# A fused attention and mixture-of-experts kernel: gathers of the second expert block behind two scatters, and a new engine order of the last six pairs and the first expert block

## The chip, the cores and the metric

The kernel runs on one core of a Trainium2 chip. The metric is the device time of one launch in microseconds (us), given as the median of several runs. One further execution was recorded by the hardware profiler; its rows are what the prediction argues from. Five engines work side by side, each with its own list of instructions: PE multiplies matrices, ACT (Activation) and DVE (Vector) work on elements, POOL (GpSimd) does the same and issues the gathers and scatters, and SP issues the plain transfers. In the profile, PEld is PE's loading of weights.

## The reference

The reference first computes attention and then sends every token of its output through one of eight small networks ("experts"):

```python
# attention: 8 batches, 8 heads, 576 positions, 64 values per head
q_rot, k_rot = rotate(q), rotate(k)
scores = scale * q_rot @ k_rot^T
scores = scores - max(scores)
attn = exp(scores); attn = attn / (sum(attn) + 1e-9)
x = (attn @ v), reshaped to 4608 tokens of 512 values
# experts: 8 of them, 512 -> 1024 -> 512
logits = x @ w_gate + modality_bias[modality_id]
e_idx = argmax(logits, axis=1)
gate_w = softmax(logits)[e_idx]
for e in range(8):
    h = relu(x[e_idx == e] @ w1[e])
    out[e_idx == e] = gate_w * (h @ w2[e])
```

## The kernel before

**Attention.** The 64 heads are done as 32 pairs, numbered 0 to 31, four pairs to a batch. For each pair there are nine blocks of scores (jobs S0 to S8, matmuls at L472), each followed by a row minimum on DVE that also copies the scores out of PSUM (MN, L481) and an exponential on ACT (EX, L490). The exponentials are then transposed on PE (the "fills" F0 to F3, FA and FB, L495) into PSUM, and brought out of PSUM half by ACT and half by DVE (A_ and B_ jobs, L432 and L528). Then come the products with V (AVA and AVB, L553), a copy of their result on ACT (OTA, OTB), the output matmuls (OUT, L590) and their evacuation on DVE (EVA, EVB, L603 to L607). A pair's jobs reach over some three periods, so that PE works on two or three pairs at once.

**PSUM.** There are four slots of two banks, ps0 to ps3. A job takes the slot that a table names for it, or the one that came free longest ago, and so a job in written order can only start when the slot's last reader has read it.

**Routing.** After the last pair of a batch the routing steps RK0 to RK14 find each token's expert (on PE one short group of matmuls, RK8 at L675 and L677, and small steps on ACT, DVE and POOL), and five scatters SC0 to SC4 on POOL write the tokens' numbers into a table in device memory (TAB<-VAL, L708).

**Experts.** Tokens are handled in blocks of 256. Eight blocks of the first plan hold tokens of batches 0 to 4 only, so that they can begin before the last batches are routed; ten more and a half block follow. For each block SP reads the block's list of tokens (ix and xi), POOL gathers the rows (8 gathers per block, XG0 or XG1 by turns, L970, in the job rows), DVE and ACT transpose and split them (tr, te, L1015), ACT and DVE split the weights (hi, lo, hi2, lo2), and PE does the two layers (l1 at L1034, l2 at L1053).

**What sets the order.** All of it is a list of small jobs. Each job has a key, and the list is sorted by key plus 14.438 times the pair's number. The table KEYS holds the keys that are the same for all pairs, EDGE replaces them pair by pair, and MOE holds the keys of the first expert blocks, relative to pair 31. PE, ACT, DVE and POOL execute their instructions in exactly the order that the sorted list gives, and so does SP until the list ends; nothing is put in another order later. After the list the rest of the expert blocks follow in an order that the code writes out (chain). A second small table, AFTER, ties five gathers of the first block to matmuls of pair 30: two to the first half of its product with V, two to the second half and one to its output matmuls. So these gathers are issued as PE gets on.

In the new kernel the lines of the code stand 18 lines further down: L472 is L490 there, L495 is L513, L553 is L571, L590 is L608, L675 is L693, L708 is L726, L970 is L988, and L1034 is L1052.

Of the kernel before, what the change touches and what calls it, by code (L numbers as in the profile page):

```python
# [84 lines left out]
        -104.800, "OTA": -100.434, "A_F3": -91.502, "B_F3": -82.128, "AVB": -67.882, "RI": -64.058, "OTB": -58.510, "OUT": -54.919,  # L85
        "EVA": -46.469, "EVB": -43.282,
    },
# [9 lines left out]
        "BIAS": -0.898, "EVA": 4.373, "EVB": 9.686, "RK0": 17.329,  # L97
    },
# [9 lines left out]
    },  # L108
# [5 lines left out]
    },  # L114
    6: {
        "LD1": -117.371, "T1": -115.739, "LD": -91.534, "T2": -87.025, "R": -60.217, "HI": -56.245, "LO": -39.229, "SWH": -29.499,
        "SWL": -25.629,
    },
    7: {
        "LD": -77.705, "LD1": -51.155, "T1": -45.849, "T2": -29.455,  # L120
    },
    8: {
        "LD1": -42.214,
    },
    19: {
        "SC3": 113.825, "SC2": 128.215, "SC4": 152.075,
    },
    23: {
        "RK6": 45.016, "RK7": 49.391, "RK8": 52.824, "RK9": 58.160, "RK10": 79.988, "RK11": 109.721, "RK12": 128.347, "RK13": 128.956,
        "RK14": 129.684, "SC3": 130.859, "SC4": 132.359, "SC2": 132.942, "SC1": 136.961, "SC0": 137.506,  # L130
    },
    25: {
        "RE": 11.575, "F2": 13.246, "A_F2": 14.351, "B_F2": 14.486, "RI": 16.427, "AVB": 18.725, "OTB": 20.519, "OUT": 26.426, "EVB":
        26.591, "EVA": 30.118,
    },
# [57 lines left out]
    },  # L193
}
MOE = dict(
    setdma=(-353.070, -199.654, -64.082, -129.156),
    consts=(28.166, 28.282),
    plan=(-34.727, 11.672, -5.857, -25.884),
    ix=(-13.525, 11.677, 11.679, 11.775),
    w1=(-33.501, -27.735, 15.231, -22.655),  # L200
    w2=(-4.011, 1.762, 12.647, -8.483),
    hi=(-22.046, 1.027, 19.870, 16.903),
    lo=(17.011, 6.975, 21.263, 19.523),
# [1224 lines left out]
```

## Time and profile before

| what | us |
|---|---|
| median of the three runs | 916.37 |
| lowest and highest of the three | 913.91 and 916.81 |
| time of the profiled execution | 911.67 |
| its span from the first to the last instruction | 909.9 |
| PE busy in that span | 863.7 (95%) |
| DVE busy | 685.8 (75%) |
| ACT busy | 632.3 (69%) |
| POOL busy | 641.1 (70%) |

The mean clock that PE was granted in the span is 0.985 of full speed. The profiled execution's own time is 1.8 us above its span. A row of the timeline gives the start, the duration, the engine, the line of the code, the operation, the result and its sources, and the number of instructions that were put together; in brackets stands the time that the engine was idle before it and what ended that time. "issue" there means that the engine waited for nothing that the profile shows. A row of the windows gives the busy time of PE, PEld, DVE, ACT and POOL in one stretch (with the number of instructions), PE's granted clock, the share of the DMA engines' time and the rate in GB/s.

### The profile page before, as it was taken

How to read it: one execution, taken by the hardware profiler on the slowest of the kernel's cores; microseconds unless marked ns; L12 is line 12 of the kernel's file. 1: busy time of each engine (PE TensorE's matmuls, PEld its weight loads, DVE VectorE, ACT ScalarE, POOL GpSimd, SP SyncE). 2: the span in 40 equal slices, each digit the busy share in tenths (PEclk: the TensorE clock that was granted, in tenths of full speed). 3: DMA queues.
4: the chain of work that ended last, by engine and by line, in shares of the span. 5: the costliest groups of instructions: out<-in, count | busy, mean ns of one | idle time of the engine just before them, and what ended most of it. 6: DMA issues, size and time to landing. Idle time of an engine off the chain costs nothing. (4 is left out here: it accounts for less than half of the span.)

```text
span 909.9 us, 25743 instructions
## 1 busy us (share of the span) xinstructions
PE 863.7 (95%) x9696; PEld 715.4 (79%) x9696; DVE 685.8 (75%) x1515; ACT 632.3 (69%) x1291; POOL 641.1 (70%) x494
## 2 busy tenths in 40 slices
PE   2899999999999999999869989999999999999996
PEld 2677777777777777777648978889999999999995
DVE  7788889888888889888739767857676666666672
ACT  2888988888988988989734545556556555555563
POOL 3999988998889999995551776765666666666401
PEclk9999999999999999999969999999999999999999
DMA  8675778788797787867601611116717112511250
GB/s 263 200 225 156 247 180 219 182 207 204 151 246 181 190 207 182 230 166 215 171 21 67 222 49 46 54 59 228 237 55 229 47 47 88 192 46 38 81 171 20
DMA packets 82465, 136.90 MB, mean 150 GB/s; under 512 B 28795, under 2 KB 53517, under 8 KB 81308
## 3 DMA queue, kind: packets, MB, share of 16 engines
q1 hardware_dynamic: 71740, 114.08, 46.5%
q0 software_dynamic: 9248, 19.46, 6.6%
q8 instruction: 78, 1.28, 0.6%
q10 hardware_dynamic: 1344, 1.62, 0.6%
q14 instruction: 55, 0.45, 0.2%
HBM read 138.16 MB, written 19.51 MB: 173 GB/s over the span
## 5 line engine op out<-in xcount | busy, mean ns | idle before, releaser
L481 DVE CUSTOM_DVE_ANT_1 sc<-ps,ZERO 128x576 f32<-128x576 f32 x288 | 206.8, 749 | 23.3 <-PE ps L472 13.0
L490 ACT ACTIVATE P<-sc,mn 128x576 f32<-128x576 f32 x288 | 219.7, 767 | 5.8 <-DVE mn L481 5.2
L970 POOL DMA_INDIRECT XG<-X,iy x148 | 174.6, 1180 | 48.5 <-issue 37.6
L1034 PE MATMUL psH<-HL,W1H 128*128 128x256 f32 x1088 | 194.6, 281 | 3.2 <-issue 2.9
L472 PE MATMUL ps<-SW 64*128 64x288 f32 x960 | 170.3, 312 | 15.8 <-DMA SW<-HL 14.9
L472 PE MATMUL ps<-HL 64*128 64x288 f32 x960 | 170.6, 311 | 3.2 <-DVE ri L573 1.1
L1034 PEld LDWEIGHTS psH<-HL,W1H 128*128 128x128 f32 x1088 | 168.1, 189 | 4.0 <-issue 1.9
L1034 PE MATMUL psH<-HL,W1L 128*128 128x256 f32 x544 | 152.8, 281 | 0.9 <-issue 0.9
L472 PEld LDWEIGHTS ps<-SW 64*128 64x128 f32 x960 | 136.2, 190 | 20.6 <-DMA SW<-HL 15.9
L429 DVE TENSOR_TENSOR W1L<-ST,W1H 128x1024 fp32r<-128x1024 f32 x76 | 90.3, 1222 | 76.3 <-ACT W1H L432 65.5
L472 PEld LDWEIGHTS ps<-HL 64*128 64x128 f32 x960 | 136.2, 190 | 8.6 <-issue 5.5
L553 PE MATMUL ps<-PH,V 128*64 128x320 f32 (+1 forms) x1024 | 140.9, 416 | 2.2 <-issue 1.2
L1057 POOL DMA_INDIRECT out_dram<-sc,ix x36 | 47.0, 1305 | 115.3 <-ACT sc L1056 94.0
L495 PEld LDWEIGHTS ps<-idf,P 64*128 64x128 f32 x2624 | 96.8, 139 | 32.7 <-ACT P L490 12.1
L432 ACT ACTIVATE PH<-ps 128x512 f32<-128x512 f32 (+1 forms) x160 | 85.3, 551 | 48.5 <-PE ps L495 25.0
L528 DVE COPY PH<-ps 128x512 f32<-128x512 f32 (+1 forms) x160 | 98.4, 630 | 26.6 <-remote 12.8
L495 PE MATMUL ps<-idf,P 64*128 64x64 f32 x2624 | 109.1, 226 | 6.9 <-issue 3.5
L1053 PE MATMUL psY<-W2L,SW 128*128 128x512 f32 x288 | 113.7, 395 | 0.0
L1053 PE MATMUL psY<-W2H,SW 128*128 128x512 f32 x288 | 112.3, 390 | 0.0
L553 PEld LDWEIGHTS ps<-PH,V 128*64 128x64 f32 x1024 | 69.7, 137 | 51.3 <-issue 6.0
L449 POOL TENSOR_TENSOR HL<-ST,HL 128x1152 fp32r<-128x1152 f32 x31 | 82.4, 2657 | 36.6 <-ACT HL L432 36.5
L1034 PEld LDWEIGHTS psH<-HL,W1L 128*128 128x128 f32 x544 | 102.9, 189 | 3.8 <-issue 3.7
(216 smaller groups left out, 1596.7 us busy)
## 6 DMA issues: line engine op xcount, KB each, us to landing
ST<-in_moe_w_dram SPq DMA_DIRECT2D x152, 512.0 KB
ST<-in_qk_dram SPq DMA_DIRECT2D x62, 576.0 KB
SW<-HL SPq DMA_DIRECT2D x124, 216.0 KB
V<-in_v_dram SPq DMA_DIRECT2D x32, 256.0 KB
X<-X SPq DMA_DIRECT2D x8, 1024.0 KB
XG<-X,iy POOLq DMA_INDIRECT x148
V<-in_v_dram SPq DMA_DIRECT2D x64, 16.0 KB
X<-XT SPq DMA_DIRECT2D x16, 64.0 KB
```

What stands on the lines that cost most here:

```text
L429: nc.vector.tensor_tensor(o, a, b, op=ALU.subtract)
L432: return nc.scalar.activation(o, i, AF.Copy, scale=scale)
L449: e.tensor_tensor(d["HL"][:, 1, o], a, d["HL"][:, 0, o].bitcast(F32), op=ALU.subtract)
L472: nc.tensor.matmul(ps[:, g, 0:288], t[:, wq, q0:q0 + P], t[:, wk, k0:k0 + 288], start=(m == 0), stop=(m == len(L) - 1))
L481: nc.vector.tensor_tensor_reduce(sc, d.pop(("S", u))[:, :, 0:288], ZERO.unsqueeze(2).to_broadcast([P, 2, 288]), 1.0, FMAX, ALU.add, ALU.mi ...
L490: nc.scalar.activation(p, sc.rearrange("p a b -> p (a b)"), AF.Exp, bias=mn, scale=-1.0, accum_out=d["sum"][:, u:u + 1])
L495: nc.tensor.transpose(ps[:, g, c:c + 64], src[r, k0:k0 + P], idf[r, r])
L528: alone(d["at", f], g, (nc.vector.tensor_copy if g else acopy)(o, i).ins)
L553: i = nc.tensor.matmul(pa[hh * 64:hh * 64 + 64, 0:c1 - c0], d["V"][:, hh, kt, :], r, start=(kt == 0), stop=(kt == 4))
L970: inst = nc.gpsimd.indirect_dma_start(out=XG[s % 2][:, t, g, :], out_offset=None, in_=X.rearrange("n (i f) -> (n i) f", f=P)[0:rows], in_o ...
L1034: l1_[s] = nc.tensor.matmul(ps[:, i, :], w[:, c, f0:f0 + P], x[:, c, :], start=(m == 0), stop=(m == 11)).ins
L1053: nc.tensor.matmul(ps, hx[:, c, t * P:(t + 1) * P], x[:, c, :], start=(m == 0), stop=(m == 23))
```

## The change

The change is one of tables, with one small change of code.

- In EDGE the numbers of pairs 0 to 22 are printed with more digits and are the same. Those of pair 23 (its routing steps), 24 (two), 25 and all of 26 to 31 are new, and so PE, ACT, DVE and POOL run these pairs' jobs in another order. The first job that differs is near the start of pair 26's scores, which PE works on at about 364 us of the profiled span.
- In MOE the eight gathers of the second expert block (rows 8 to 15) go from keys 11.78 to 14.07 to keys 17.36 to 17.43, which is behind two scatters of batch 5 (SC3 and SC4 of pair 23). What they read, the block's list of tokens (plan 1, ix 1), goes from 11.67 to 16.18 and 17.30. The steps of the first block (hi, lo, tr, te, hi2, lo2, l1, l1e) have new keys too.
- `alone` declares that two users of one slot that work in different banks of it need not wait for each other. It now gets the half of the pair that each of them belongs to, and leaves the dependence in place where the half is the same.

On SP the order of the transfers is kept, but for the second block's plan and list, which now stand behind two weight loads, and the stores of the last batch, which stand behind two more. POOL issues the same gathers and scatters. Nothing is added and nothing removed: each engine has the same instructions.

The core of the diff (of the tables two or three lines each):

```diff
     31: {
-        "LD": -37.174, "T2": -35.339, "LD1": -34.769, "T1": -28.480, "R": -24.189, "HI": -20.952, "LO": -14.069, "SWL": -13.658, "SWH":
...
+        "LD": -37.17400, "LD1": -34.76900, "T2": -34.16480, "T1": -26.03419, "R": -22.15154, "HI": -21.41976, "LO": -19.21119, "SWL":
...
 MOE = dict(
-    plan=(-34.727, 11.672, -5.857, -25.884),
-    ix=(-13.525, 11.677, 11.679, 11.775),
+    plan=(-34.72700, 16.18300, -5.85700, -25.88400),
+    ix=(-13.52500, 17.30000, 11.67900, 11.77500),
...
-    rows=(5.189, -7.595, 2.778, 1.170, -0.984, 8.071, 5.429, 11.766, 11.780, 11.790, 14.020, 14.030, 14.040, 14.050, 14.060, 14.070,
+    rows=(5.18900, -7.59500, 2.77800, 1.17000, -0.98400, 8.07100, 5.42900, 11.76600, 17.36000, 17.37000, 17.38000, 17.39000, 17.40000,
...
-    def alone(own, b, inst):
+    def alone(own, b, inst, part=None):
 
-        for x, i in use[own]:
-            if x != b and i.engine != inst.engine:
+        for x, p, i in use[own]:
+            if x != b and i.engine != inst.engine and (p is None or p != part):
                 tc.declare_no_dep(inst, i, reason="two banks")
-        use[own].append((b, inst))
+        use[own].append((b, part, inst))
...
-            alone(d["at", f], g, (nc.vector.tensor_copy if g else acopy)(o, i).ins)
+            alone(d["at", f], g, (nc.vector.tensor_copy if g else acopy)(o, i).ins, int(f[1] in "23B"))
...
-                alone(own, half, i.ins)
+                alone(own, half, i.ins, half)
```

How the instructions stand at the two places that the prediction rests on is shown here. A row has the line, the operation, the result and its sources with their numbers, the size, and how often the instruction follows itself.

On PE, the end of pair 31's scores, before. P0 and P1 hold pair 31's exponentials, of which the rows at L495 are fills F1 and F0; oT is pair 30's product with V, and the rows at L675 are the first ones of RK8 of batch 6:

```order
L472 MATMUL ps3_130<-SW1_85 128x288
L495 MATMUL ps1_128<-idf_65,P1_119 128x64 x16
L590 MATMUL ps0_127<-RW_112,oT0_113 64x72 x18
L495 MATMUL ps3_130<-idf_65,P0_118 128x64 x16
L675 LDWEIGHTS UT_146
L675 MATMUL ps1_128<-OH_148,UT_146 128x48
```

and the same place on PE in the new kernel:

```order
L490 MATMUL ps0_127<-SW1_85 128x288
L513 MATMUL ps3_130<-idf_65,P0_118 128x64 x16
L608 MATMUL ps1_128<-RW_112,oT0_113 64x72 x18
L693 LDWEIGHTS UT_146
L693 MATMUL ps2_129<-OH_148,UT_146 128x48
```

Before, RK8 follows fills F1, OUT of pair 30 and fill F0, in slot ps1, which held F1; now it follows F0 and OUT of pair 30, in slot ps2, and F1 comes after it.

On POOL, the gathers of the first and second expert block (XG0 and XG1) and the scatters into the table, before:

```order
L970 DMA XG0_75<-X_63,iy_8540 128x128 x4
L962 TENSOR_SCALAR iy_8994<-xi_8981,CF_70 128x8
L970 DMA XG1_76<-X_63,iy_8994 128x128 x2
L689 TENSOR_TENSOR rk_8906<-rk_8906,OH_148 128x40
L970 DMA XG1_76<-X_63,iy_8994 128x128 x6
L697 CAST oi_9063<-of_9041 128x5
L708 DMA TAB_64<-VAL_71,oi_9063 41472x2 x5
```

and in the new kernel:

```order
L988 DMA XG0_75<-X_63,iy_8581 128x128 x7
L715 CAST oi_8986<-of_8709 128x5
L726 DMA TAB_64<-VAL_71,oi_8986 41472x2 x2
L980 TENSOR_SCALAR iy_9110<-xi_9108,CF_70 128x8
L988 DMA XG1_76<-X_63,iy_9110 128x128 x8
L726 DMA TAB_64<-VAL_71,oi_8986 41472x2
L638 COPY G_149<-BI_144 128x5x8
L726 DMA TAB_64<-VAL_71,oi_8986 41472x2 x2
L707 TENSOR_TENSOR rk_8882<-rk_8882,OH_148 128x40
```

Before, eight gathers of XG1 go ahead of all five scatters, and before them stand four gathers of XG0 in a row, the other four being issued further up, between small routing steps; now seven gathers of XG0 stand in a row, two scatters follow, then the eight gathers of XG1, and then the other three scatters.

More of the change, by code (lines that the diff above doesn't have):

```diff
@@ L115 @@
-    6: {
-        "LD1": -117.371, "T1": -115.739, "LD": -91.534, "T2": -87.025, "R": -60.217, "HI": -56.245, "LO": -39.229, "SWH": -29.499,
-        "SWL": -25.629,
[6 rows of a table added]
+        -378.64700, "LV": -364.17600, "FB": -346.46500, "A_FB": -336.88000, "B_FB": -329.74400, "AVA": -327.20100, "OTA": -302.11700,
+        "F3": -299.87500, "A_F3": -295.07300, "B_F3": -294.95300, "AVB": -234.67400, "OTB": -230.71800, "RI": -224.64500, "OUT":
+        -153.22800, "EVA": -132.78200, "EVB": -119.48400,
+    },
[9 rows of a table added]
+        -196.83900, "AVA": -190.98200, "OTA": -176.51300, "RE": -145.24400, "AVB": -140.63700, "RI": -126.46800, "OTB": -111.27300,
+        "OUT": -65.54500, "EVA": -42.99700, "EVB": -41.82000,
+    },
[8 rows of a table added]
+        "B_F2": -118.63100, "RE": -114.64700, "B_FB": -114.13100, "A_FB": -113.59600, "AVA": -109.96600, "F3": -104.80000, "OTA":
+        -100.43400, "A_F3": -91.50200, "B_F3": -82.12800, "AVB": -67.88200, "RI": -64.05800, "OTB": -58.51000, "OUT": -54.91900, "EVA":
+        -46.46900, "EVB": -43.28200,
+    },
[8 rows of a table added]
+        "FB": -51.27500, "A_FB": -49.23100, "AVA": -45.36800, "B_F2": -42.94200, "B_FB": -42.19100, "F3": -41.92200, "OTA": -41.65200,
+        "A_F2": -39.41600, "A_F3": -38.58300, "B_F3": -34.37400, "RE": -34.12100, "RI": -14.32900, "AVB": -13.48900, "OTB": -8.26400,
+        "OUT": -1.34400, "BIAS": -0.89800, "EVA": 4.37300, "EVB": 9.68600, "RK0": 17.32900,
+    },
[9 rows of a table added]
+        "AVB": 14.42600,
+    },
[6 rows of a table added]
+    },
@@ L118 @@
+    6: {
+        "LD1": -117.37100, "T1": -115.73900, "LD": -91.53400, "T2": -87.02500, "R": -60.21700, "HI": -56.24500, "LO": -39.22900, "SWH":
+        -29.49900, "SWL": -25.62900,
     },
     7: {
-        "LD": -77.705, "LD1": -51.155, "T1": -45.849, "T2": -29.455,
+        "LD": -77.70500, "LD1": -51.15500, "T1": -45.84900, "T2": -29.45500,
     },
     8: {
-        "LD1": -42.214,
+        "LD1": -42.21400,
     },
     19: {
-        "SC3": 113.825, "SC2": 128.215, "SC4": 152.075,
+        "SC3": 113.82500, "SC2": 128.21500, "SC4": 152.07500,
@@ L127 @@
     },
     23: {
-        "RK6": 45.016, "RK7": 49.391, "RK8": 52.824, "RK9": 58.160, "RK10": 79.988, "RK11": 109.721, "RK12": 128.347, "RK13": 128.956,
-        "RK14": 129.684, "SC3": 130.859, "SC4": 132.359, "SC2": 132.942, "SC1": 136.961, "SC0": 137.506,
+        "RK5": 40.90127, "RK6": 46.67389, "RK7": 57.40156, "RK8": 64.29648, "RK9": 67.61357, "RK10": 82.92576, "RK11": 85.53740, "RK12":
+        96.07624, "RK13": 114.20615, "RK14": 128.57076, "SC3": 130.85900, "SC4": 132.35900, "SC2": 132.94200, "SC1": 136.96100, "SC0":
@@ L131 @@
+        137.50600,
+    },
+    24: {
+        "EVB": 25.99150, "EVA": 26.06138,
     },
     25: {
-        "RE": 11.575, "F2": 13.246, "A_F2": 14.351, "B_F2": 14.486, "RI": 16.427, "AVB": 18.725, "OTB": 20.519, "OUT": 26.426, "EVB":
-        26.591, "EVA": 30.118,
+        "AVA": 10.88958, "FB": 12.15678, "B_FB": 13.12055, "OTA": 13.19636, "F2": 13.31092, "B_F2": 13.52622, "A_FB": 14.37274, "RE":
+        14.41030, "A_F2": 14.56559, "F3": 14.92462, "A_F3": 15.78341, "B_F3": 16.11466, "AVB": 16.75621, "RI": 18.17626, "OTB":
+        20.01352, "OUT": 27.50939, "EVB": 29.53316, "EVA": 29.76110,
@@ L135 @@
     },
     26: {
[5 rows of a table removed]
-        "OTB": 24.647, "RI": 27.870, "OUT": 31.453, "EVA": 32.577, "EVB": 35.739,
[6 rows of a table added]
+        "AVA": 13.37242, "B_F2": 14.18103, "OTA": 15.10887, "AVB": 20.37058, "OTB": 22.17156, "RI": 30.50016, "OUT": 33.13718, "EVA":
+        33.71284, "EVB": 36.68954,
     },
     27: {
[5 rows of a table removed]
-        "A_FB": 13.315, "B_FB": 14.059, "AVA": 14.280, "RE": 14.638, "A_F3": 14.844, "B_F3": 15.844, "OTA": 16.826, "AVB": 19.635,
[3 rows of a table removed]
[6 rows of a table added]
+        15.84080, "FB": 15.97787, "AVA": 16.14316, "A_FB": 16.77823, "OTA": 16.82819, "B_FB": 17.62644, "AVB": 20.22011, "OTB":
@@ L154 @@
+        21.83520, "OUT": 25.12055, "EVB": 25.68147, "EVA": 25.70549, "BIAS": 26.59725, "RK0": 27.27627, "RK1": 30.31245, "XO": 36.25000,
+        "RK2": 40.37238, "RK3": 43.17076, "RK4": 44.57894, "RK5": 48.83850, "RK6": 56.47619, "RK7": 56.55748, "RK8": 66.74962, "RK9":
+        67.91421, "RK10": 75.41390, "RK11": 81.11650, "RK12": 81.45284, "RK13": 82.49673, "RK14": 82.51116, "SC0": 83.05200,
     },
     28: {
[6 rows of a table removed]
-        "OTA": 17.939, "RE": 19.181, "AVB": 20.414, "OTB": 23.398, "RI": 25.977, "OUT": 38.336, "EVA": 39.257, "EVB": 40.186,
[7 rows of a table added]
@@ L163 @@
+        16.05280, "B_F3": 16.56402, "AVB": 19.82456, "OTB": 24.47882, "RI": 28.16419, "OUT": 37.99977, "EVA": 38.80736, "EVB": 40.35017,
     },
     29: {
[6 rows of a table removed]
-        "B_FB": 12.181, "OTA": 12.576, "RE": 12.876, "B_F3": 13.074, "RI": 13.187, "A_F3": 13.894, "AVB": 15.303, "OTB": 20.667, "OUT":
-        40.409, "EVA": 46.235, "EVB": 48.346,
[8 rows of a table added]
+        "EVB": 53.24566, "EVA": 53.43772,
     },
     30: {
[7 rows of a table removed]
-        21.050, "OUT": 21.663, "EVA": 37.670, "EVB": 37.831,
[7 rows of a table added]
+        12.05367, "A_F3": 12.41287, "B_F2": 12.87059, "A_FB": 13.34276, "B_FB": 14.29187, "AVB": 18.71721, "RE": 18.88984, "OTB":
@@ L183 @@
+        19.15819, "RI": 19.30164, "OUT": 22.05238, "EVB": 26.15506, "EVA": 32.21461,
     },
     31: {
[6 rows of a table removed]
-        12.309, "F2": 12.476, "B_FB": 12.480, "A_F2": 12.738, "AVA": 13.069, "B_F2": 13.586, "AVB": 16.396, "OTB": 23.586, "OTA":
-        23.807, "OUT": 24.531, "RI": 24.900, "EVA": 24.910, "EVB": 24.920,
[7 rows of a table added]
+        13.65186, "A_F3": 14.42523, "AVA": 15.43182, "AVB": 15.76070, "RE": 17.38437, "OTB": 18.55238, "OTA": 19.95731, "BIAS":
+        20.75437, "OUT": 24.42589, "RI": 24.90000, "EVA": 24.91000, "EVB": 24.92000,
@@ L195 @@
 MOE = dict(
-    setdma=(-353.070, -199.654, -64.082, -129.156),
-    consts=(28.166, 28.282),
-    plan=(-34.727, 11.672, -5.857, -25.884),
-    ix=(-13.525, 11.677, 11.679, 11.775),
[L200 to L203, printed above, removed]
-    tr=(13.315, 14.512),
-    te=(14.739, 14.961),
-    hi2=(19.097, 17.808, 17.228, 16.018),
-    lo2=(24.633, 22.805, 24.459, 19.614),
-    l1=(17.301, 17.002, 22.720, 21.734),
-    l1e=(22.809, 22.869, 24.662, 24.647),
-    w1n=(20.502, 24.643, 23.254, 22.825),
-    place=(10.490, 11.490),
-    rows=(5.189, -7.595, 2.778, 1.170, -0.984, 8.071, 5.429, 11.766, 11.780, 11.790, 14.020, 14.030, 14.040, 14.050, 14.060, 14.070,
-        25.150, 25.160, 25.170, 25.180, 25.190, 25.200, 25.210, 25.220),
-    pl=(-114.356, -102.856, -99.906, -88.406, -85.506, -73.956, -51.417, -48.907, -45.303),
+    setdma=(-353.07000, -199.65400, -64.08200, -129.15600),
+    consts=(28.16600, 28.28200),
+    plan=(-34.72700, 16.18300, -5.85700, -25.88400),
+    ix=(-13.52500, 17.30000, 11.67900, 11.77500),
+    w1=(-33.50100, -27.73500, 15.23100, -22.65500),
+    w2=(-4.01100, 1.76200, 12.64700, -8.48300),
+    hi=(-19.90978, 15.80757, 21.38490, 15.44691),
+    lo=(6.12812, 16.23179, 22.24599, 20.18067),
+    tr=(11.97182, 13.67190),
+    te=(14.33785, 14.80071),
+    hi2=(20.51992, 16.30432, 17.29412, 16.03064),
+    lo2=(23.20071, 17.00040, 22.32476, 20.98521),
+    l1=(15.78498, 17.03336, 23.35045, 22.37281),
+    l1e=(21.32014, 23.18167, 23.40073, 22.43414),
+    w1n=(20.50200, 24.64300, 23.25400, 22.82500),
+    place=(10.49000, 11.49000),
+    rows=(5.18900, -7.59500, 2.77800, 1.17000, -0.98400, 8.07100, 5.42900, 11.76600, 17.36000, 17.37000, 17.38000, 17.39000, 17.40000,
+        17.41000, 17.42000, 17.43000, 25.15000, 25.16000, 25.17000, 25.18000, 25.19000, 25.20000, 25.21000, 25.22000),
+    pl=(-114.35600, -102.85600, -99.90600, -88.40600, -85.50600, -73.95600, -51.41700, -48.90700, -45.30300),
     end=25.0,
```

7 lines of the change are left out of this document (removed), and 158 rows, old and new, of the table EDGE.

## The prediction

> **What bounds the kernel now.** The busy times of the page come first, then the chain of waits, to see from where on the end is fixed.
>
> ```profile
> PE 863.7 (95%) x9696; PEld 715.4 (79%) x9696; DVE 685.8 (75%) x1515; ACT 632.3 (69%) x1291; POOL 641.1 (70%) x494
> 575.75 11.36 PE psH L1034 x95
> 587.11 11.10 PE psY L1053 x48
> ...
> 877.28 11.10 PE psY L1053 x48
> ```
>
> PE is busy for 863.7 of 909.9 us, and from 575.75 us the chain is PE alone, one expert block after the other in 11.2 + 11.1 us. Nothing that the change moves stands there, so the end comes earlier only by as much as PE reaches 575.75 earlier. I therefore looked for PE's losses in the windows of the part that the change reorders, from about 364 us on.
>
> ```profile
> 364.00:420.00 56.00, 55.59 (x908) 42.77 (x910) 47.97 (x145) 49.67 (x131) 52.45 (x42) 1.00 0.74 196
> 420.00:440.00 20.00, 19.46 (x298) 14.41 (x296) 16.53 (x46) 18.52 (x48) 5.18 (x8) 1.00 0.74 199
> 440.00:445.00 5.00, 3.94 (x54) 2.88 (x51) 3.39 (x12) 2.66 (x8) 3.93 (x7) 1.00 0.79 209
> 445.00:450.00 5.00, 5.00 (x54) 3.27 (x56) 4.36 (x12) 4.36 (x11) 3.29 (x4) 1.00 0.51 117
> 450.00:455.00 5.00, 3.15 (x102) 2.74 (x100) 2.83 (x8) 3.45 (x11) 3.20 (x4) 1.00 0.75 241
> 455.00:460.00 5.00, 3.08 (x45) 2.04 (x39) 2.13 (x6) 1.25 (x4) 3.91 (x6) 0.60 0.19 47
> 460.00:465.00 5.00, 1.90 (x12) 1.25 (x11) 0.27 (x2) 0.00 (x0) 3.81 (x6) 0.50 0.18 48
> 465.00:470.00 5.00, 2.51 (x14) 1.30 (x14) 0.00 (x0) 0.00 (x0) 3.79 (x4) 0.50 0.02 1
> 470.00:475.00 5.00, 4.69 (x27) 3.50 (x29) 2.87 (x4) 3.42 (x5) 0.00 (x0) 0.70 0.01 0
> 475.00:480.00 5.00, 5.00 (x42) 4.41 (x39) 4.97 (x10) 5.00 (x6) 0.00 (x0) 1.00 0.00 0
> ```
>
> Up to 440 us PE is full (55.59 of 56.00, 19.46 of 20.00). After it there are short losses and then, from 455 to 475 us, a large one: PE is busy for 12.18 of 20 us, at a granted clock of 0.60, 0.50, 0.50 and 0.70. Busy time multiplied by clock is 1.85 + 0.95 + 1.26 + 3.28 = 7.3 us of full work, so some 12.7 us are lost. The waits, of the window from 440 to 476.5 us (engine, line, what it waited for, us in total, times, longest) and, in the last row, of PE from 364 to 440, say to what the losses are put down:
>
> ```profile
> PE ps L495 <- issue: 3.5, 6, 1.0
> PE ps L590 <- issue: 3.0, 6, 1.1
> PE ps L675 <- ACT PH L432: 1.8, 1, 1.8
> PE ps L553 <- issue: 1.2, 2, 0.9
> PE ps L472 <- DVE ri L573: 1.1, 1, 1.1
> ACT PH L432 <- remote: 14.0, 2, 12.4
> ...
> PE ps L472 <- ACT PH L432: 0.5, 1, 0.5
> ```
>
> Three waits name another engine: 1.8 (RK8), 1.1 and 0.5 us, 3.4 in all. The other 7.7 us (3.5 + 3.0 + 1.2) are "issue": PE waits for nothing that the profile shows. ACT is idle 12.4 us in one piece meanwhile, for it needs PE's next fill, so ACT doesn't hold PE. What runs beside this stretch is POOL's list:
>
> ```profile
> 444.34 0.26 POOL L661 TENSOR_TENSOR vv<-vv,vm 128x40 f32<-128x40 f32 x1
> ...
> 448.69 1.00 POOL L970 DMA_INDIRECT XG<-X,iy  x1 [0.30 <-issue]
> 451.13 0.99 POOL L970 DMA_INDIRECT XG<-X,iy  x1 [1.45 <-PE ps L590]
> 452.76 1.06 POOL L970 DMA_INDIRECT XG<-X,iy  x1 [0.27 <-POOL iy L962]
> ...
> 462.12 0.99 POOL L970 DMA_INDIRECT XG<-X,iy  x1 [0.30 <-issue]
> 463.60 1.03 POOL L708 DMA_INDIRECT TAB<-VAL,oi  x1 [0.28 <-issue]
> ...
> 468.74 0.97 POOL L708 DMA_INDIRECT TAB<-VAL,oi  x1 [0.30 <-issue]
> ```
>
> and PE's own:
>
> ```profile
> 450.51 0.86 PE L590 MATMUL ps<-RW,oT 64*64 64x72 f32 x36
> 451.33 0.72 PE L495 MATMUL ps<-idf,P 64*128 64x64 f32 x16
> 453.88 0.20 PE L675 MATMUL ps<-OH,UT 128*128 128x48 bf16 x1 [1.83 <-ACT PH L432]
> 453.92 0.27 PE L677 MATMUL ps<-OH,ON 128*128 128x40 bf16 x5
> ...
> 456.28 0.53 PE L590 MATMUL ps<-RW,oT 64*64 64x72 f32 x5 [0.37 <-issue]
> ...
> 471.37 2.06 PE L553 MATMUL ps<-PH,V 128*64 128x256 f32 x9 [0.31 <-issue]
> ...
> 476.47 0.50 PE L1034 MATMUL ps<-HL,W1H 128*128 128x256 f32 x2
> ```
>
> POOL issues gathers and scatters without a break from 451.13, the last gather of XG0, which waits for OUT of pair 30, to 469.71. PE's "issue" holes begin 5.2 us after 451.13 and end 1.7 us after the last scatter. That they lie together is all that the trace shows; the cause stays open, and my cases differ in what they make of it.
>
> **The change part by part.** *RK8 of batch 6.* Before, it stands behind fill F0 and takes the slot of F1, and so it waits until F1's halves are out of PSUM. ACT's part of that is late:
>
> ```profile
> 452.73 1.09 ACT L432 ACTIVATE PH<-ps 128x512 f32<-128x512 f32 x2 [0.55 <-PE ps L495]
> ```
>
> Two copies take ACT from 452.73 to 453.82, and RK8 starts at 453.88. Now RK8 takes ps2, which fill FA held several jobs earlier, and stands behind OUT of pair 30, 0.86 us long. I count the 1.8 us as gone; bounds 0 (something else comes last there) and 1.8.
>
> *The two short waits*, 1.1 and 0.5 us, belong to scores whose slot was not read out yet. The new order puts other jobs there and moves DVE's reciprocal of pair 30 (ri), at which the longer one ended, behind the reading of four more scores. I take both as gone, 1.6 us; bounds are 1.6 gained and 1.6 lost, since the order of six pairs may make as much of new waiting as it takes away: 364 to 440 shows how little is left to gain (0.41 + 0.54 us).
>
> *A new wait.* Fill F2 of pair 31 now comes right after RK8, in ps0, the slot of the last scores (S6), and needs DVE to have read them; FB needs their exponential. On DVE the split lo of the first weights now stands directly ahead of that reading. The nearest rows, from the timeline of DVE and from the groups of 440 to 476.5 us, are
>
> ```profile
> 449.09 1.22 DVE L429 TENSOR_TENSOR W1L<-ST,W1H 128x1024 fp32r<-128x1024 f32 x1
> L481 DVE CUSTOM_DVE_ANT_1 sc<-ps,ZERO 128x576 f32<-128x576 f32 x6 | 4.4, 754 | 0.8 <-PE ps L472 0.6 <-ACT oT L432 0.2
> L490 ACT ACTIVATE P<-sc,mn 128x576 f32<-128x576 f32 x8 | 6.1, 767 | 0.6 <-DVE mn L481 0.6
> ```
>
> If lo begins as the scores end, DVE has read them 1.22 + 0.75 = 2.0 us later; PE by then has done F0 (0.72), OUT (0.86) and RK8 (0.3, from 453.88 to 454.19), 1.9 us, and waits 0.1. The exponential ends at 2.0 + 0.77 = 2.8, or 3.0 behind another on ACT, and PE reaches FB after two more fills, at 1.9 + 0.1 + 1.4 = 3.4: no wait. I take 0.1 lost; bounds 0 and 1.2 (the whole of lo). Behind this wait stand PE's fills F2, F1 and FB, and for these ACT and DVE wait.
>
> That subtraction and a gather overlap here: DVE runs from 449.09 to 450.31, POOL's gather from 448.69 to 449.69, at 1.22 and 1.00 us as elsewhere. [...]
>
> *The gathers of XG1* stand behind two scatters, each a step of about 1.3 us (463.60 to 468.74 is four steps), so 2.6 us later. They ended at 463.1 before. They are needed here:
>
> ```profile
> L1015 DVE STREAM_TRANSPOSE XG<-XG x2: 659/676/692, 492.7 to 493.4; 128x512 f32<-128x512 f32 x2
> ```
>
> 27 us of slack cover it: 0 us. Without the cover (a stall of POOL of that length) each later microsecond would delay the second block by one. The three scatters left behind serve tables that are read later still; 0 as well. SP's order changes for one list and some stores, with 2.6 us of delay under the same slack: 0. Splits and transposes of the first block stand earlier on ACT and DVE, but the block waits for PE, which goes from the last product with V straight on at 476.47: 0.
>
> *The stall.* After OUT of pair 30 PE has the same work left as before (F2, F1, FB, OUT of pair 29, F3, both products), in another order, and POOL the same fourteen transfers (one gather, eight gathers, five scatters). I leave its 12.7 us as they are; bounds are the rivals.
>
> Sum: 1.8 + 1.1 + 0.5 - 0.1 = 3.3 us. The profiled execution took 911.67 us, its span 909.9; the span becomes 906.6, the time about 908.4. It is 4.7 below the median shown, 916.37, so the same difference taken off the median gives **913.0 us**.
>
> **The rivals.** *The stall goes or shrinks.* If the fault lies in how these jobs follow each other on PE and not in POOL's list, another order may dissolve it: up to 12.7 us more come back, to some 900 us; half of it gives 907. For it speaks that no wait on POOL is shown; against it that the number of jobs and transfers behind OUT of pair 30 is the same.
>
> The granted clock fell to 0.50 only after PE had been mostly idle, and was 1.00 again from 475. [...]
>
> *Nothing moves.* If PE's stall ends with POOL's last scatter and POOL's list starts with OUT of pair 30, then only what is saved ahead of OUT counts, at most the 1.6 us; RK8's 1.8, behind OUT, is swallowed by the stall. That gives 914.8, and 916.4 where new waits eat the 1.6. For it: PE is free 1.7 us after the last scatter, with no other work of POOL behind.
>
> *Slower: the stall begins earlier.* Before, four gathers of XG0 are issued ahead of or right at the routing step vv of POOL (444.34), spread out over the time in which PE was full, and four behind it. Now only one stands ahead of vv, and seven come behind it in a row. vv waits for a routing step on DVE. If that is late, POOL's unbroken string begins while PE still has scores, fills and OUT of pair 30 to do, and is five transfers longer, 5 x 1.3 = 6.5 us. From 455 to 470 PE did 4.06 us of full work in 15, a loss of 73%: 4.7 us, so 916.4 + 4.7 = 921.1. It decides from the point where PE's first "issue" hole lies ahead of OUT of pair 30. Against it: three of the seven gathers are tied to matmuls of pair 30 as before, and spread as PE gets on.
>
> **How the numbers follow.** A measurement of this kernel can tell about 0.3%, 2.75 us, from no change. The forecast (3.3 us, its own range 910.5 to 914) has 0.34, the stall that goes or shrinks 0.10, no change 0.27, and the longer stall, with new waits in the reordered pairs that cost as much, 0.29. The forecast is only just over the bound. So faster 0.44, same 0.27, slower 0.29. A range that holds eight in ten leaves out most of the first rival's whole gain and the last part of the slow case: 905 to 922.
>
> **What would show it.** Right: RK8's row without a wait, PE idle for other engines under 0.5 us between 440 and 455, first matmul of the first block (L1052 now) at about 473, and the "issue" rows of the three lines still near 7.7 us. Nothing moves: that matmul at 475 or later although RK8 doesn't wait. Stall gone: granted clock 1.00 throughout, the first block at about 461. Longer stall: "issue" holes ahead of OUT of pair 30, clock below 1.00 in more than the four windows here, first block at 480 or later. Wrong in all cases would be a difference that arises behind the first expert block, or ahead of 420 us.

## The result, and the profile after

The changed kernel takes 977.43 us (median of four runs, 970.31 to 981.83) against 915.14 us of the kernel before on the same chip: **1.069 times** as long, 95% interval 1.060 to 1.078. The forecast was 913 us, the range 905 to 922. The profiled execution took 970.31 us, its span is 968.5 us. The runs of this study fell on several chips, on which the kernel before takes between 884 and 916 us, so only runs that shared a chip are compared, and ratios are given where chips differ.

The busy times of the changed kernel, from its page:

```profile
PE 883.3 (91%) x9696; PEld 717.3 (74%) x9696; DVE 688.5 (71%) x1515; ACT 638.0 (66%) x1291; POOL 638.3 (66%) x494
```

The work is the same and every engine's share has fallen: all of them wait more. Where, is told by the windows. Here are two stretches of attention that the prediction left aside, before:

```profile
100.00:200.00 100.00, 99.41 (x1640) 76.10 (x1638) 86.25 (x260) 87.81 (x228) 88.98 (x54) 1.00 0.76 191
200.00:300.00 100.00, 98.51 (x1584) 74.08 (x1582) 85.09 (x255) 87.78 (x228) 90.86 (x59) 1.00 0.84 198
```

and after, with the first stretch that the prediction looked at (364 to 420 us, where PE was busy for 55.59 us before):

```profile
100.00:200.00 100.00, 89.57 (x1400) 65.14 (x1396) 75.19 (x228) 78.35 (x197) 75.28 (x47) 1.00 0.66 167
200.00:300.00 100.00, 89.27 (x1402) 65.36 (x1400) 74.52 (x220) 76.84 (x195) 79.02 (x50) 1.00 0.80 176
364.00:420.00 56.00, 50.58 (x782) 36.59 (x780) 42.43 (x129) 44.00 (x111) 44.72 (x35) 1.00 0.67 176
```

PE's share falls from 99% to 89%, evenly, from the first pairs on, in pairs whose keys are the same digit for digit, at a granted clock of 1.00. PE did 1400 matmul records from 100 to 200 us where it did 1640, 15% fewer. So it is no matter of the last six pairs. The waits from 100 to 364 us say what it is. Before (the two largest rows):

```profile
ACT PH L432 <- PE ps L495: 18.7, 35, 1.1
DVE PD L528 <- PE ps L495: 17.3, 15, 1.3
```

and after:

```profile
DVE PH L546 <- ACT PH L450: 29.1, 34, 1.5
...
ACT PH L450 <- DVE PH L546: 21.4, 13, 1.7
DVE PD L546 <- ACT PD L450: 18.7, 12, 1.6
PE ps L513 <- ACT PH L450: 18.5, 16, 1.5
```

Before, the copies that bring a fill out of PSUM (PH and PD, on ACT and DVE) waited for PE, as they must. Now ACT's copies wait for DVE's and DVE's for ACT's, and PE's fills wait for the copies. The timeline shows one such place. Before, the two engines copy side by side (a row each of ACT and of DVE):

```profile
197.38 1.10 ACT L432 ACTIVATE PH<-ps 128x512 f32<-128x512 f32 x2
```

```profile
197.70 1.28 DVE L528 COPY PH<-ps 128x512 f32<-128x512 f32 x2
```

After, one stands behind the other (rows of DVE, ACT, DVE and PE, by time):

```profile
217.98 0.68 DVE L546 COPY PH<-ps 128x512 f32<-128x512 f32 x1
```

```profile
218.75 1.09 ACT L450 ACTIVATE PH<-ps 128x512 f32<-128x512 f32 x2 [1.69 <-DVE PH L546]
```

```profile
219.87 0.69 DVE L546 COPY PH<-ps 128x512 f32<-128x512 f32 x1 [1.22 <-ACT PH L450]
```

```profile
219.40 0.71 PE L513 MATMUL ps<-idf,P 64*128 64x64 f32 x16 [1.20 <-ACT PH L450]
```

ACT waits 1.69 us for DVE, then DVE 1.22 us for ACT, and PE 1.20 us until a slot is free. This comes back once a pair: 16 times in the row of PE above, one for each of the 16 or 17 pairs that fit in these 264 us.

The reason stands in `alone`. It is called for each copy with the half that the fill belongs to. The ACT copy and the DVE copy of *one* fill belong to the same half, so the new condition (p is None or p != part) doesn't only keep a product with V tied to the copies of its half; it also no longer declares the two copies of a fill free of each other. They write interleaved columns of one tile. In the listed order, the waits of DVE's 256 copies show it (the first row before, the second after, for the same instruction):

```
L528 COPY PH_125<-ps_130 128x8x64 [waits PE_49]
L546 COPY PH_125<-ps_130 128x8x64 [waits Activation_49]
```

Of DVE's 256 copies 34 wait for ACT before, and 154 after.

The end of attention has the stall as before on this chip. From the windows and the waits of 480 to 550 us after:

```profile
515.00:520.00 5.00, 2.59 (x27) 1.42 (x26) 2.62 (x6) 1.38 (x3) 3.78 (x5) 0.58 0.35 41
520.00:525.00 5.00, 1.90 (x13) 1.29 (x13) 0.00 (x0) 1.64 (x4) 3.78 (x5) 0.50 0.20 52
525.00:530.00 5.00, 1.76 (x12) 1.42 (x13) 0.00 (x0) 0.00 (x0) 3.38 (x5) 0.50 0.07 14
```

```profile
PE ps L608 <- issue: 4.7, 7, 1.0
PE ps L490 <- DVE PD L546: 4.4, 1, 4.4
PE ps L513 <- issue: 4.0, 7, 0.9
...
PE ps L1052 <- DVE HX L1061: 1.8, 1, 1.8
...
PE ps L693 <- DVE PD L546: 0.9, 1, 0.9
```

The stall is there again, with 8.7 us of "issue" (7.7 before); RK8 (L693) waits 0.9 us instead of 1.8, now for a copy on DVE, and there are two long waits that weren't there before: 4.4 us ahead of scores, and 1.8 us within the first expert block. The first matmul of the first expert block comes at 538.40 us instead of 476.47, so that the loss arises ahead of the expert blocks.

### The profile page after: what moved, and what is told of

It reads as the page before. It is cut to its first block, busy times and chain, and to the rows that moved or that the text cites. A ratio compares the mean times of both kernels' runs of the same rounds, so it can differ in the third digit from the quotient of the medians.

```text
span 968.5 us, 25638 instructions
## 1 busy us (share of the span) xinstructions
PE 883.3 (91%) x9696; PEld 717.3 (74%) x9696; DVE 688.5 (71%) x1515; ACT 638.0 (66%) x1291; POOL 638.3 (66%) x494
## 4 chain that ended last, share of the span: by engine, by line
PE 76%; DVE 9%; ACT 8%; issue 4%; DMA 2%; another core or an unknown queue 1%; ACTq 0%; POOLq 0%; POOL 0%; DVEq 0%
PE psY L1071 21%; PE psH L1052 20%; PE ps L571 16%; PE ps L490 9%; DVE PH L546 6%; PE ps L513 5%; ACT PH L450 4%; PE ps L608 3%; ACT P L508 2%; DVE PD L546 1%; PE ps L1052 1%; DVE sc L499 1%; ACT PD L450 1%; DMA SW<-HL 1%
## 5 line engine op out<-in xcount | busy, mean ns | idle before, releaser
L988 POOL DMA_INDIRECT XG<-X,iy x148 | 177.2, 1197 | 56.7 <-issue 37.2
L490 PE MATMUL ps<-SW 64*128 64x288 f32 x960 | 184.2, 318 | 21.4 <-DMA SW<-HL 14.3
L1052 PE MATMUL psH<-HL,W1H 128*128 128x256 f32 x1088 | 191.3, 279 | 0.0
L490 PE MATMUL ps<-HL 64*128 64x288 f32 x960 | 185.0, 318 | 3.6 <-DVE PH L546 1.2
L546 DVE COPY PH<-ps 128x512 f32<-128x512 f32 (+1 forms) x160 | 100.8, 634 | 83.4 <-ACT PH L450 42.9
L490 PEld LDWEIGHTS ps<-HL 64*128 64x128 f32 x960 | 138.2, 190 | 14.8 <-DVE mn L499 5.6
L513 PE MATMUL ps<-idf,P 64*128 64x64 f32 x2624 | 111.5, 227 | 33.2 <-ACT PH L450 22.9
```

The lines of the kernel that those rows point to most:

```text
L490: nc.tensor.matmul(ps[:, g, 0:288], t[:, wq, q0:q0 + P], t[:, wk, k0:k0 + 288], start=(m == 0), stop=(m == len(L) - 1))
L513: nc.tensor.transpose(ps[:, g, c:c + 64], src[r, k0:k0 + P], idf[r, r])
L546: alone(d["at", f], g, (nc.vector.tensor_copy if g else acopy)(o, i).ins, int(f[1] in "23B"))
L988: inst = nc.gpsimd.indirect_dma_start(out=XG[s % 2][:, t, g, :], out_offset=None, in_=X.rearrange("n (i f) -> (n i) f", f=P)[0:rows], in_o ...
L1052: l1_[s] = nc.tensor.matmul(ps[:, i, :], w[:, c, f0:f0 + P], x[:, c, :], start=(m == 0), stop=(m == 11)).ins
```

## The experiments

**Theory 1** is that the loss is the new rule in `alone`, by making the two copies of one fill exclude each other. **Rival 2** is that the order of the last six pairs makes it. The remainder, a few us, belongs to the first expert block (**theory 3**) or to the pairs' order.

### The new rule alone

The kernel before with the new `alone` and its two calls, and nothing else:

```diff
-            if x != b and i.engine != inst.engine:
+            if x != b and i.engine != inst.engine and (p is None or p != part):
```

> The kernel before with nothing but the new rule in alone; all tables as before. Theory 1 (the ACT half and the DVE half of one fill carry the same half-number, so under the new rule they are no longer declared free of each other, and each fill's second evacuation waits for its first): nearly the whole loss is here, 960 to 985 us, PE about 90% busy between 100 and 364 us instead of 99%, and waits of DVE's PH copies for ACT's and back of some 80 us. Rival 2 (the new order of the last six pairs makes the loss): 912 to 918 us, no such waits.

Measured: 946.27 us against 884.43, ratio 1.068 (1.065 to 1.071). The window and three rows of the waits from 100 to 364 us:

```profile
100.00:364.00 264.00, 237.24 (x3594) 170.70 (x3594) 193.67 (x577) 201.17 (x504) 198.45 (x125) 0.97 0.68 168
```

```profile
DVE PH L528 <- ACT PH L432: 27.9, 33, 1.5
ACT PH L432 <- DVE PH L528: 26.8, 16, 2.0
DVE PD L528 <- ACT PD L432: 24.9, 13, 3.2
```

With all keys as before, the whole loss is there: +61.8 us, PE at 90%, and 79.6 us of copies waiting for copies. Rival 2 is out. The absolute time lies below the range that was written, since this chip takes 884 us for the kernel before and not 915; the difference was expected at 45 to 70.

### The changed kernel with the copies free of each other

```diff
-            if x != b and i.engine != inst.engine and (p is None or p != part):
+            if x != b and i.engine != inst.engine and (p is None or p != part or mybir.EngineType.PE not in (i.engine, inst.engine)):
```

> The changed kernel with one condition more in alone: the dependence of the same half is kept only where one of the two is PE, so the two evacuations of one fill are free of each other as before, and PE's product with V still waits for the evacuations of its half. All new tables stay. Theory 1: 905 to 922 us (the prediction's sum would make it 913), PE 99% busy between 100 and 364 us. Rival 2: still above 960 us.

Measured: 888.82 us against 884.43, ratio 1.0047 (1.0029 to 1.0065).

```profile
100.00:364.00 264.00, 262.44 (x4290) 199.79 (x4286) 227.55 (x684) 233.21 (x602) 240.69 (x156) 1.00 0.79 197
```

PE is back at 99%. All but 4.4 us of the loss is the exclusion of the copies; 4.4 us are left, and of the forecast gain nothing is seen. Here too the time lies below the range that was written, for a chip of 915 us. The new rule wasn't taken out altogether: in the new order products with V stand in a slot beside copies of their own half, whose results they read, and that dependence stays. No run has the new order without it, so its cost can't be told from the rest of the 4.4 us.

### Before and after on one chip

The kernel before, unchanged, and the changed kernel, unchanged, once more.

> The kernel before, unchanged, for its profile on the chip of these runs. If PE's stall behind OUT of pair 30 belongs to the kernel, it shows again: 7.7 us of issue time, granted clock 0.50 to 0.70 from 455 to 475 us, about 915 us. If it belongs to the chip or the execution: about 884 us, no such stall, first matmul of the first expert block at about 456 instead of 476 us.

> The changed kernel, unchanged, on the chip of these runs. Theory 1 (the evacuations of one fill exclude each other, and this costs nearly everything): 1.07 times the kernel before on this chip too, some 945 to 952 us if that takes 884, with PE at about 90% from 100 to 364 us. If part of the 62 us was the stall of the first chip's executions: a ratio under 1.05.

Measured: 885.31 us in one run of the kernel before (median of the 17 on this chip: 884.86), and 949.14 us of the changed one, ratio 1.073 (1.070 to 1.076), as theory 1 had it. The window from 100 to 364 us, before and after on this chip:

```profile
100.00:364.00 264.00, 262.58 (x4292) 199.93 (x4290) 228.03 (x686) 233.40 (x603) 240.89 (x156) 1.00 0.82 197
```

```profile
100.00:364.00 264.00, 235.94 (x3688) 172.25 (x3688) 198.03 (x588) 205.46 (x516) 204.62 (x130) 1.00 0.70 172
```

Here the whole difference can be laid out from the two timelines (spans 883.5 and 944.1 us, +60.6). The first matmul of the first expert block comes at 513.99 instead of 457.23: +56.8, of which PE's idle time in this window alone makes 26.6 us (262.58 - 235.94). From there to the first matmul of its second layer it takes 15.91 instead of 12.19: +3.7. The rest, to the end, takes 414.2 instead of 414.1.

PE's idle time is not the whole of the 56.8 us. Up to the first expert block, before and after:

```profile
0.00:457.20 457.20, 435.55 (x6982) 332.38 (x6982) 388.40 (x1134) 388.62 (x989) 393.09 (x286) 1.00 0.78 201
```

```profile
0.00:513.90 513.90, 453.30 (x6982) 332.75 (x6982) 392.26 (x1135) 393.21 (x985) 391.28 (x286) 1.00 0.68 178
```

For the same 6982 matmuls PE is idle for 60.6 us instead of 21.7 (+39), and busy for 17.8 us more. Most of the second part is in the scores: their matmuls are about as long as before (316 ns in the mean against 312, and on the first chip 318 against 312) but start further apart, and the row of those from HL is busy for 183.9 us instead of 170.6 (185.0 instead of 170.6 on the first chip). So the busy share shows too little of the loss: from 100 to 364 us it falls by 10%, and the number of matmuls (4292 to 3688) by 14%.

And the kernel before has no stall behind OUT of pair 30 here:

```profile
455.00:460.00 5.00, 5.00 (x41) 3.75 (x38) 4.97 (x10) 5.00 (x7) 4.13 (x3) 1.00 0.10 28
460.00:465.00 5.00, 5.00 (x45) 5.00 (x44) 4.33 (x6) 1.90 (x4) 4.68 (x3) 1.00 0.06 16
465.00:470.00 5.00, 5.00 (x71) 4.70 (x70) 4.85 (x10) 1.29 (x4) 4.39 (x3) 1.00 0.06 13
```

PE is full at clock 1.00 while POOL issues the same gathers and scatters. The stall doesn't belong to the kernel alone. That it belongs to the chip, and not to something else in which the groups of runs differed, isn't shown.

### Which copies cost what

Two kernels free one kind of copies only: the first those of F0 to F3, the second those of FA and FB (the call of `alone` gets one more argument, shown for the first).

```diff
-            alone(d["at", f], g, (nc.vector.tensor_copy if g else acopy)(o, i).ins, int(f[1] in "23B"))
+            alone(d["at", f], g, (nc.vector.tensor_copy if g else acopy)(o, i).ins, int(f[1] in "23B"), f[1] in "0123")
```

> The changed kernel, but only the evacuations of fills F0 to F3 are freed of each other; those of FA and FB still exclude each other. If the loss goes with the time of the second copies (four of about 0.6 us against one of 0.3 and one of about 0.9 per pair), a third of the loss stays: 905 to 912 us where the evacuations all exempt took 889. If PE only suffers from the large copies: 889 to 894. If FB, which stands right ahead of the product with V, makes the loss: over 930.

Measured: 909.65 us, ratio 1.026 (1.023 to 1.030); FA and FB make 909.65 - 888.82 = 20.8 us, a third of the loss, as the time of their copies had it. PE's largest row of waits there, from 100 to 364 us, and the window:

```profile
PE ps L513 <- DVE PH L546: 9.3, 16, 0.6
```

```profile
100.00:364.00 264.00, 250.14 (x4044) 189.89 (x4038) 213.28 (x648) 219.59 (x566) 224.88 (x142) 0.99 0.75 183
```

The wait per pair is 0.6 us instead of 1.2. PE's share is half way between, but 4.0 us of its idle time there are two waits that the profile puts down to "issue" (one of 3.7 us); without them a third of the lost share is left, as of the time.

> The counterpart of the run with fills F0 to F3 exempt: the changed kernel with only the evacuations of FA and FB freed of each other, those of F0 to F3 still excluding each other. If the two parts add up: FA and FB cost 909.65 - 888.82 = 20.8 us, so 949.1 - 20.8 = 928 us here, some 39 us over all exempt. If they overlap (one late copy hides the other): under 922 or over 934.

This one fell on a chip on which the kernel before takes 912.7 us, so the 928 us are not comparable; the expected ratio is 928 / 884.9 = 1.049. Measured: 960.6 us, ratio 1.054 (1.045 to 1.063). The parts add up within the interval: taken as differences from the ratio of the run with all free (1.0047), FA and FB make 0.022 and F0 to F3 0.049, 0.071 in all, and the whole is 0.069 (1.0734 - 1.0047). The interval leaves out the case under 922 us (a ratio of 1.042), but not the one over 934 (1.055), so that a small overlap of the two parts isn't ruled out.

### The gathers' place

Two kernels: the kernel before with only plan 1, ix 1 and the eight gathers moved, and the changed kernel with the copies free and these put back. The first:

```diff
-    plan=(-34.727, 11.672, -5.857, -25.884),
-    ix=(-13.525, 11.677, 11.679, 11.775),
+    plan=(-34.727, 16.183, -5.857, -25.884),
+    ix=(-13.525, 17.300, 11.679, 11.775),
...
-    rows=(5.189, -7.595, 2.778, 1.170, -0.984, 8.071, 5.429, 11.766, 11.780, 11.790, 14.020, 14.030, 14.040, 14.050, 14.060, 14.070,
+    rows=(5.189, -7.595, 2.778, 1.170, -0.984, 8.071, 5.429, 11.766, 17.360, 17.370, 17.380, 17.390, 17.400, 17.410, 17.420, 17.430,
```

> The kernel before with only the second block's plan, list and eight gathers moved behind two scatters, as in the change. The prediction's term is 0: within 2 us of before, and the stall of PE after OUT of pair 30 stays at about 7.7 us of issue time. Rival (the stall of PE is made by the eight gathers following the last gather of the first block at once): the stall begins some 2.6 us later or is shorter, 2 to 6 us faster. Rival (gathers late for the second block): slower by over 2 us, with a wait of DVE's transpose at the second block.

> As the run with the evacuations exempt, but with the second block's plan, list and gathers at their old keys. If the gathers' place is worth nothing: the same time as that run within 2 us. If the new order was made for the gathers behind two scatters and needs it: slower than that run by 2 to 8 us, with PE's issue holes beginning earlier.

Measured: 886.75 us, ratio 1.0023 (1.0003 to 1.0044), and 888.24 us, ratio 1.0042 (1.0023 to 1.0061; with the gathers moved it was 1.0047). In the new order their place is worth nothing that can be measured. In the old order the move loses 2.3 us, with an interval from 0.3 to 3.9 us: there the gathers come too late for the second block, as the timelines of POOL, DVE and PE show:

```profile
458.51 5.24 POOL L970 DMA_INDIRECT XG<-X,iy  x1 [0.31 <-issue]
```

```profile
477.55 0.71 DVE L1015 STREAM_TRANSPOSE XG<-XG 128x512 f32<-128x512 f32 x1 [4.28 <-DMA XG<-X,iy]
```

```profile
481.38 0.50 PE L1034 MATMUL psH<-HL,W1H 128*128 128x256 f32 x2 [1.37 <-ACT W1H L432]
```

A gather of 5.24 us (what runs beside it is told at the end) holds the six behind it, DVE's transpose waits 4.28 us for the last ones, and PE waits 1.37 us for weights that ACT splits after it, and 0.82 us more for DVE's part. The rival that the eight gathers make the stall by following the first block's last gather at once could not be tested by this run, for its chip shows no stall. Against it stands the profile after on the first chip: two scatters lie between them there, and the stall is the same.

### The first expert block

With the copies free, the order of the read-outs l1e was changed in two steps; first those of groups 1 and 3 behind the last group's matmuls, then only that of group 3:

```diff
-    l1e=(21.32014, 23.18167, 23.40073, 22.43414),
+    l1e=(21.32014, 23.38000, 23.40073, 23.37000),
```

```diff
+    l1e=(21.32014, 22.28000, 23.40073, 23.37000),
```

> All evacuations exempt as before, and two steps of the first expert block (the read-outs l1e of groups 1 and 3) in written order behind the last group's matmuls. Theory 3: in the new order the last group (2) is written behind the read-out of group 3, which works in the other bank of the same slot, and so PE waits 1.83 us for it and then runs at a lower clock; before, it wasn't. Then the first block's first layer takes 12.2 us again instead of 15.8, and the time falls by 2 to 4 us against the run with the evacuations exempt, to about the kernel before. Rival: the wait moves to the second layer, which needs the read-outs, and nothing is gained.

> All evacuations exempt, and of the first expert block's read-outs l1e only that of group 3 behind the last group's matmuls; that of group 1 stands ahead of group 3's. Theory 3 (the first layer's 1.83 us wait came from the other bank of the slot, and the second layer's 1.31 us wait in the last run from group 1's read-out standing too late): first layer plus OUT of pair 31 back at about 12.2 us, 1 to 2 us faster than that run (887), level with the kernel before (884 to 885.5). Rival: the wait moves once more, 887.

Measured: 887.07 us, ratio 1.0023 (1.0012 to 1.0035), and 886.28 us, ratio 1.0011 (0.9995 to 1.0028), after 1.0047 with neither. In the profile of the kernel with neither, the last group's matmuls look like this:

```profile
469.16 0.52 PE L1052 MATMUL ps<-HL,W1H 128*128 128x256 f32 x2 [1.83 <-DVE HX L1061]
...
469.69 0.63 PE L1052 MATMUL ps<-HL,W1H 128*128 128x256 f32 x2
```

HX is what DVE's part of l1e writes. Group 2 works in the other bank of the slot of group 3, and stands behind group 3's read-out in the list, so it waits for it. In the first of the two kernels this wait is gone and another one of 1.31 us has come at the second layer, which needs group 1's read-out; in the second one both are gone. First matmul of the first layer to first of the second: 15.84, 13.76 and 12.32 us, and 12.19 in the kernel before. Theory 3 holds as far as the wait goes. In time the second step is 0.8 us where 1 to 2 were expected, and 886.28 us lies just above the expected 884 to 885.5; the intervals of the two kernels overlap, and the second one's includes 1, no change against the kernel before.

### RK8's slot, and the pairs' order alone

In the kernel before, only the slot that RK8 of batch 6 asks for:

```diff
+            SLOTS["RK8"] = 6 if b == 6 else 5
             own, bk = take("RK8", None)
```

> The kernel before with one slot changed: RK8 of batch 6 takes ps2 instead of ps1; the fills behind it move to other slots, the order of jobs stays. The prediction's largest term by itself: RK8 doesn't wait for F1's copies any more. If the wait was worth its length (1.25 us in the profile of the kernel before on this chip): 1 to 1.3 us faster. If the next fill waits for the same copies instead: within 0.5 us of before.

Measured: 884.91 us against 884.74, ratio 0.9996 (0.9981 to 1.0010). RK8 has no wait any more, and the next fill has one:

```profile
450.67 1.16 PE L495 MATMUL ps<-idf,P 64*128 64x64 f32 x30 [1.00 <-ACT PH L432]
```

The slot that RK8 leaves is the one that the next fill takes, and this waits for the same copies: 1.25 us of RK8 in the kernel before have become 1.00.

Last, the changed kernel with the copies free and the whole table MOE of the kernel before:

> The changed kernel with all evacuations exempt and the whole table of the first expert block and of the gathers as before: only the new order of pairs 23 to 31 is left. If the first block's new order makes what is left over the kernel before (4 us): within 1 us of before, 884 to 886. If the pairs' order does: 887 to 889. By the prediction's sum, with the waits that this chip's profile of before shows (1.25 us at RK8, the two others absent): 1.2 us faster.

Measured: 887.65 us, ratio 1.0031 (1.0015 to 1.0047). The 1.2 us that the prediction's sum would gain don't come. So the new order of the pairs doesn't go well with the old first block either: its first layer starts at 457.52, about where it did (457.23), RK8 still waits 1.04 us, now for a copy on DVE, and PE loses some 1.5 us in the first block's two layers. No kernel here is faster than the one before by more than the noise; the nearest changed one, with the copies free and l1e reordered, isn't told from it.

## Why the prediction was wrong

- *The bound, and where to look.* PE as the bound and the end fixed from the expert blocks on were read rightly (414.2 us against 414.1 from the second layer to the end). The step that failed is the next one: "I therefore looked for PE's losses in the windows of the part that the change reorders, from about 364 us on". The change has a part that is no reordering: `alone`, which works in all 32 pairs. The text before the prediction says what it does, and the sum puts it at nothing without a reason. So a difference ahead of 420 us, which the prediction names as a sign that all its cases are wrong, is what came. What the runs put in the place of that missing term is +61.8 us for this part by itself, where the whole change makes 64.3 on such a chip: each fill's two copies wait for each other, and PE's fills for them. Rows of the profile before gave a sign of it: of a pair's six fills four have two copies of about 0.6 and 0.69 us, which would now go one behind the other instead of side by side, on engines that are busy for 69 and 75%. How much of that PE would pay could not be read from them.
- *RK8, 1.8 us gained.* The wait was real and the step from it to the end wasn't: by itself the other slot changes nothing that can be measured (884.91 against 884.74 us, an interval of 0.9981 to 1.0010), since the next fill waits for the same copies. And in the new order something else comes last at RK8, as the lower bound allowed: a copy on DVE, for which it waits 0.9 us in the profile after and 1.04 us with only the pairs' order; with the copies free it waits 0.44 us, put down to "issue".
- *The two short waits, 1.6 us gained.* They are absent from the kernel before on the other chip (from 364 us on no wait of scores over 0.3 us), so their cause isn't the order alone. In the changed kernel on the first chip scores wait 4.4 us for a copy on DVE, and on the other chip no longer than 0.6 us. The lower bound, 1.6 us lost, was too narrow where copies are late.
- *The new wait of F2 and FB, 0.1 us.* Right: the profile shows no wait of theirs in the run with the copies free. In other rows something is long beside subtractions of L429, but there it is a gather (5.24 us) and not the subtraction (1.18 to 1.21 us for the four beside it; last section).
- *The gathers of XG1, 0 us.* Right in the new order (1.0042 and 1.0047), too small in the old one (+2.3 us). The 27 us of slack were those of an execution with the stall. Without it the first block starts 19 us earlier (457.23), and in the kernel before only 8.8 us lie between the last gather's end (464.51) and the transposes (473.3); the move takes 2.6 of them, and slow gathers (5.24 and 2.99 us) the rest.
- *The first block's splits, 0 us.* Wrong: the first layer takes 3.7 us longer. The term rests on what the first matmul waits for, and leaves out the order of read-outs between the groups.
- *The stall, left as it is.* On the chip that has it, it stays with the new order, at 8.7 instead of 7.7 us of "issue", so that the first rival is out. It is absent with the old order too, on other chips; its cause stays open. The prediction's reading that the clock fell only after PE had been mostly idle is too strong: in windows of 1 us the clock is 0.50 from 456 us on, and PE was busy for 3.08 us of the 5 us before that.
- *The slower rival* had the right sign by luck. Its cause didn't occur: in the changed kernel the "issue" holes begin behind OUT of pair 30, as before.

## What to carry to other kernels

A change that puts a dependence back, or stops declaring that there is none, is a change of every place that calls it: list the pairs of instructions that the new condition catches, and count in the listed order which instructions wait for another engine than before, ahead of any reading of moved work. Two engines that split one buffer's read-out are worth their independence: here it was 7% of the kernel. And a wait taken from one instruction is gained only if the next one doesn't need the same thing.

## What the runs showed of the hardware

The same kernel before takes 884 to 885 us (medians) on three chips, and 913 and 915 us in the other two groups of runs. On the three chips PE goes on through POOL's long string of gathers and scatters without the "issue" holes, and some of POOL's gathers take longer than 1.0 us, as here in the kernel before (timeline of POOL):

```profile
454.44 1.77 POOL L970 DMA_INDIRECT XG<-X,iy  x1 [0.30 <-issue]
...
460.04 4.47 POOL L970 DMA_INDIRECT XG<-X,iy  x1 [0.30 <-issue]
```

In the other two groups the gathers of this string take 0.99 to 1.11 us and PE is the one that comes to a halt, as in the run with FA and FB free:

```profile
505.00:510.00 5.00, 2.16 (x17) 1.49 (x16) 1.13 (x4) 2.34 (x6) 3.78 (x5) 0.50 0.20 52
510.00:515.00 5.00, 2.32 (x15) 1.32 (x16) 0.00 (x0) 0.00 (x0) 4.20 (x6) 0.50 0.11 27
```

The stall's cause stays open. What runs beside the long gathers does stand in the traces, and on the first chip too. DVE's rows beside the one of 4.47 us:

```profile
458.96 1.21 DVE L429 TENSOR_TENSOR W1L<-ST,W1H 128x1024 fp32r<-128x1024 f32 x1
...
462.43 1.21 DVE L429 TENSOR_TENSOR W2L<-ST,W2H 128x1024 fp32r<-128x1024 f32 x1
```

These are the subtractions that split the weights. Four of them follow each other from 458.96 to 463.64, and the gather that begins among them, at 460.04, ends at 464.51, 0.87 us after the last one. So it is with all of them: of the 226 gathers, scatters and indirect stores of this execution 72 take over 1.25 us; every one of these has a subtraction of L429 running 0.15 us after it begins and ends 0.79 to 0.97 us after the end of one, and none of the 130 that have no subtraction running then takes so long. In the profile before of the first chip the counts are 63 long ones, all of this kind, and none of 135. The subtractions are not lengthened (1.17 to 1.24 us; in the profile before of the first chip those of W1L and W2L take 1.20 to 1.23 us where they overlap a long gather, and 1.18 to 1.27 us where they don't). During the stall of that profile DVE has hardly any work (busy for 0.27 us from 460 to 470 us, and no subtraction of L429 between 450.31 and 473.43), and the gathers there take 0.99 to 1.06 us. This is read from traces; no run moved a subtraction to test it.

The granted clock fell after a hole of PE of 1.83 us. Windows of 1 us of the run with the copies free, around that wait:

```profile
469.00:470.00 1.00, 0.84 (x5) 0.84 (x6) 1.00 (x3) 0.00 (x0) 0.75 (x1) 0.76 0.00 0
470.00:471.00 1.00, 1.00 (x7) 1.00 (x7) 0.83 (x1) 0.00 (x0) 0.94 (x1) 0.50 0.03 1
471.00:472.00 1.00, 1.00 (x6) 1.00 (x6) 0.00 (x0) 0.00 (x0) 0.95 (x2) 0.50 0.00 0
472.00:473.00 1.00, 1.00 (x7) 1.00 (x6) 0.00 (x0) 0.00 (x0) 0.00 (x0) 0.53 0.03 1
473.00:474.00 1.00, 1.00 (x23) 0.87 (x25) 0.00 (x0) 0.18 (x1) 0.00 (x0) 1.00 0.00 0
```

The hole was followed by some 3.4 us at half clock: three matmuls of the first layer (two of W1H, one of W1L) took 0.64 us there (470.12 to 470.76) and 0.35 us ahead of the hole (459.00 to 459.35). An estimate from the windows, with PE's work going by the clock, is (1 - 0.76) + 3 - (0.50 + 0.50 + 0.53) = 1.7 us of work lost, so that the wait cost 3.5 us, close to the 3.65 us by which the first layer was longer. Holes of 1.25 us (RK8 in the kernel before; mean clock 1.00 from 440 to 460 us) and 1.31 us (the second layer in the run with l1e later; 1.00 from 460 to 480 us) left the clock at 1.00. Two waits close together, 1.37 and 0.82 us with PE busy for 0.81 of 3 us (the kernel before with only the gathers moved), were followed by a lower one: 0.91 in the mean from 480 to 500 us, with two matmuls of W1H taking 0.63 us at 483.72 and 0.40 us at 482.93.
